# Attention and expert layer on one core: batch 0's value block sums by 128 queries, and a new listed order

## The chip, the cores and the metric

The kernel runs on one core of a Trainium2 chip. Its time is the device time in microseconds (us) of one execution. The core has five engines that each work through a list of their own, in order: PE (matrix products, with weight loads of its own, PEld), DVE and ACT (elementwise work and copies), POOL (here it issues loads) and SP (here it issues stores and moves). They wait for one another through semaphores.

## The reference, cut to what matters

Four batches of eight heads, 768 positions, head dimension 64. Each query sees its neighbours closer than 16 positions, and besides them 24 blocks of 32 keys, each by the maximum of its keys and the mean of its values. An expert layer follows on the 3072 x 512 result.

```python
def _attn_ref(q, k, v):
    k_sum = k.reshape(B, H, nb, block, D).max(axis=3)
    v_sum = v.reshape(B, H, nb, block, D).mean(axis=3)
    scores_l = scale * np.matmul(q, k.transpose(0, 1, 3, 2))
    mask_l = np.abs(pos[:, None] - pos[None, :]) < window
    scores_s = scale * np.einsum('bhsd,bhnd->bhsn', q, k_sum) + np.log(block)
    scores_all = np.concatenate([np.where(mask_l, scores_l, -1e9), scores_s], axis=-1)
    a = softmax(scores_all)
    return np.matmul(a, np.concatenate([v, v_sum], axis=2))

def _moe_ref(x, w_in, w_out):
    h = x @ w_in
    g = h * np.clip(h + 3.0, 0.0, 6.0) / 6.0
    return g @ w_out
```

## The kernel before

**Attention.** Queries go in blocks of 64 (12 of them, `NQ`). The keys of a block are its window of 96 positions (`WIN`) and, below them on partitions 96 to 119, the 24 block maxima: 120 rows in all (`KEYS`). `kaug` holds these keys, `vaug` the values in the same form, `qT` the queries, turned. Scores are products into a pair of PSUM banks `S`, `exp` on ACT makes `at` of them, and a product with `vaug`, which has a column of ones beside the 64 values, gives sums and divisor at once. `normal` (line 596) divides on DVE: a reciprocal `rc`, then `xn`. Transposes on PE and a copy give `x`, the expert layer's input, one tile for each half batch.

**Batch 0** starts the kernel and differs. Its heads go in four pairs `p`. Its late queries (the half called 0, `low` maps it) are scored first. `values_first` (line 567) makes the value products of that half in two steps, so that the first needn't wait for the block sums: `values1a` with the window's values, `values1b` with the block sums, which `vsum_first` (line 527) makes on PE and copies to `vf`. Both steps take 64 queries at a time, 12 products for a pair, in the two halves of the array's columns (`c`). The other half's queries come by wider loads, `qwide` (line 326), which PE transposes at line 442 (`q2`, `q3`) and DVE or ACT copy into `qT`.

**Expert layer.** A tile of 384 rows goes through 16 columns (`f1`): four products with `win` into a bank `h`, of which there are three, a relu on ACT into `r` (line 671), and a gate on DVE (line 672) into `g`. Then `f2` multiplies `g` with `wout` in three row blocks of four parts each into a bank `o` or `h`; a copy to `ot` and a store from SP end a block. The last row block of the last tile is cut into columns of 256, 128 and 128; one of the 128 is copied by ACT (line 698) and stored from ACT's own queue (line 699).

**Order.** Nothing is scheduled by the program itself: `ORDER` is a text of 977 tokens written out in the file, and `issue` (line 134) issues one operation for each. `v02.1` is the second operation of `values_first(2)`, `F0x3.0` the first of column 3 of tile 0, `G71x256.4` an operation of row block 1 of tile 7, `s`, `k`, `q`, `u`, `h`, `w` stand for scores, keys, queries, block sums, the values ahead of a block, and the turning of batches 1 to 3. `:A` or `:D` chooses ACT or DVE. So a token's place sets the order on its engine, and the PSUM banks and buffers are dealt out in that order too. `~`, `-`, `_` and `=` are products on a tile of ones (line 778) that keep PE at work.

Of the kernel before, what the change touches and what calls it, by code (L numbers as in the profile page):

```python
# [15 lines left out]
D = 64  # L16
BLK = 32
QB = 64
PAD = 16
WIN = QB + 2 * PAD  # L20
KEYS = 120
# [10 lines left out]
q0.1:A s000.1 q0.2:A =1 s010.0 s010.1 k2.2:A k3.2:D k3.3:D k3.1 V00.0 h000.0:D h001.0:D k2.1 k2.4 s000.2 ~2 =5 v00.0 V01.0 u0.0  # L32
h010.0:D s020.0 c.16 s010.2 q1.2:A u0.3:D u0.1:D u0.4:D v01.0 v01.1 v01.2 v00.1 q1.1:A V02.0 h020.0:A h021.0:A h011.0:A v00.2
s020.1 v01.3 v00.3 V03.0 u1.0 u1.3:A h030.0:D s030.0 k3.4 ~2 s030.1 u1.4:D v01.4 h031.0:D Q0w0.0 Q0w1.0 v01.5:D Q0w2.0 =1 q3.0
q3.1:D q2.0 u1.1:A u1.2:D s020.2 v02.0 v02.1 v02.2 s021.0 v02.3 s030.2 v03.0 v03.1 q2.1:A v03.2 s011.0 v03.3 v00.4 v00.5:D
v02.4 s021.1 s011.1 s021.2 v03.4 v03.5:D s011.2 v02.5:A s031.0 s031.1 s001.0 s031.2 I2.0 F0x3.0 F0x3.1 F0x3.2 F0x3.3 F0x3.4
F0x3.5 I4.0 F0x6.0 F0x6.1 F0x6.2 F0x4.0 F0x4.1 F0x4.2 F0x4.3 v411.0 v411.1 F0x5.0 F0x4.4 F0x4.5 v411.2 s001.1 I8.0 u0.2:A
s001.2 F0x8.0 F0x8.1 F0x8.2 F0x5.1 I0.0 F0x5.2 F0x11.0 F0x1.0 F0x11.1 F0x11.2 F0x1.1 F0x1.2 F0x1.3 F0x1.4 F0x1.5 v410.0 v410.1
F0x7.0 F0x7.1 F0x7.2 v410.2 F0x10.0 F0x10.1 I12.0 F0x13.0 F0x13.1 F0x15.0 F0x15.1 F0x13.2 F0x10.2 v411.3 v411.4:D v410.3
v410.4:A F0x15.2 F0x14.0 F0x14.1 F0x14.2 F0x9.0 F0x9.1 F0x9.2 F0x0.0 F0x0.1 F0x2.0 F0x2.1 K13.0 K10.0 c.12:A F0x0.2 K12.0 K11.0  # L40
w10.0 Q1w1.0 F1x14.0 F1x14.1 F1x14.2 F1x4.0 F1x4.1 F1x4.2 F1x2.0 F1x2.1 F1x2.2 w10.1:D F0x2.2 F0x2.3 F0x2.4 F0x12.0 F0x12.1
F0x12.2 F1x8.0 F1x8.1 F1x8.2 F1x1.0 F1x1.1 F1x1.2 F0x0.3 F0x0.4 F0x0.5 F0x2.5 F1x9.0 F1x9.1 F1x9.2 F1x5.0 F1x5.1 F1x5.2 F1x15.0
F1x15.1 w11.0 w11.2 F1x15.2 w11.3:D Q1w4.0 Q1w2.0 Q1w0.0 w10.2 w10.3:D q6.0 q6.1:A q7.0 q7.1:A F1x7.0 F1x7.1 w11.1:A F1x7.2
# [12 lines left out]
w22.1 v110.3 v110.4:A F2x7.0 F2x7.1 G11x0.2 F3x14.0 F3x14.1 F2x14.2 F2x7.2 F3x14.2 s200.0 s200.1 w23.1 w21.5:A s200.3 G11x0.3
F3x9.0 F3x9.1 F3x9.2 F3x8.0 F3x8.1 F3x8.2 F3x13.0 Q31.0 K31.0 s200.4 s200.2 G11x0.4:A G11x0.5 G12x0.5 s210.0 s210.3 s210.4
s210.1 s210.2 F3x4.0 F3x12.0 G22x0.0 F3x13.1 F3x13.2 H3.0 v201.0 K32.0 V32.0 w20.5:D F3x4.1 F3x4.2 V30.0 G00x0.5 F3x12.1 v200.0
v200.1 F3x2.0 v201.1 v201.2 v201.3 G22x0.1 F3x0.0 F3x0.1 G22x0.2 G22x0.3 w23.5:A G22x0.4:A F3x12.2 v200.2 v200.3 v201.5 F3x1.0
F3x1.1 F3x1.2 s201.0 w31.0 G20x0.0 v201.4 F3x0.2 F3x2.1 s201.3 F3x2.2 F3x11.0 s201.1 G20x0.1 F3x5.0 F3x11.1 F3x3.0 F3x5.1  # L60
F3x11.2 w30.0 F3x5.2 v201.7 F3x15.0 G20x0.2 F3x15.1 F3x15.2 w30.3 F3x3.1 F3x3.2 w22.5:A w30.4:D s201.4 F3x6.0 F3x6.1 H3.1:A
G20x0.3 G20x0.4:A F3x7.0 F3x10.0 G21x0.0 s211.0 F3x7.1 F3x10.1 s201.2 F3x7.2 s211.3 s211.1 F3x10.2 w32.0 F3x6.2 w32.3 s211.4
s211.2 w30.2:A G21x0.1 G21x0.2 G21x0.3 G21x0.4:A u6.0 u6.1:D u6.5:A u6.4:A u6.2:A w31.3 v211.0 v201.6 v210.0 v210.1 v210.2
w31.2:D v211.1 v210.3 v211.2 v211.3 G10x0.5 w31.4:D w33.0 G32x0.0 G32x0.1 G32x0.2 G32x0.3 G32x0.4:A F4x14.0 F4x14.1 F4x14.2
F4x4.0 F4x4.1 w32.2:A F4x4.2 F4x15.0 F4x15.1 F4x15.2 w31.1 G30x0.0 G30x0.1 F4x8.0 F4x8.1 F4x8.2 F4x2.0 F4x2.1 F4x2.2 F4x13.0
G30x0.2 F4x13.1 u6.3:A F4x13.2 w33.3 F4x7.0 F4x7.1 F4x7.2 G21x0.5 G20x0.5 v211.4 F4x6.0 F4x6.1 F4x6.2 v211.7 v211.6 v211.5
w30.1 F4x11.0 F4x11.1 F4x11.2 G30x0.3 G30x0.4:A G30x0.5 F4x1.0 F4x1.1 w33.2:A F4x1.2 w32.4:D F4x5.0 F4x5.1 F4x5.2 G22x0.5
# [95 lines left out]
def kernel(  # L163
# [74 lines left out]
    def bank(b, i=0):  # L238
        return b.slot[:, i] if any(b.slot is x for x in pairs) else b.slot[:]
# [570 lines left out]
```

## Time and profile before

| what | us |
|---|---|
| median of 3 runs | 216.8 |
| lowest and highest run | 216.46, 218.23 |
| span of the profiled execution, first to last instruction | 214.9 |
| PE busy in it | 208.8 |
| DVE busy | 162.7 |
| ACT busy | 135.9 |

The span is 1.9 us below the median of the runs, which also hold what lies around the first and last instruction; the profiled execution has no time of its own beside its span. Busy time of PE counts from the start of a product to its modelled end, and products overlap, so the spacing of their starts tells more than a mean length. A stretch's row gives its length, then busy time and count for PE, PEld, DVE, ACT and POOL, then the granted clock of PE, the load on the DMA engines and GB/s. A row of the timeline gives start, length, engine, line, what is written from what, and in brackets how long the engine stood idle before it and for whom.

### The profile page before, as it was taken

How to read it: one execution, taken by the hardware profiler on the slowest of the kernel's cores; microseconds unless marked ns; L12 is line 12 of the kernel's file. 1: busy time of each engine (PE TensorE's matmuls, PEld its weight loads, DVE VectorE, ACT ScalarE, POOL GpSimd, SP SyncE). 2: the span in 40 equal slices, each digit the busy share in tenths (PEclk: the TensorE clock that was granted, in tenths of full speed). 3: DMA queues.
4: the chain of work that ended last, by engine and by line, in shares of the span. 5: the costliest groups of instructions: out<-in, count | busy, mean ns of one | idle time of the engine just before them, and what ended most of it. 6: DMA issues, size and time to landing. Idle time of an engine off the chain costs nothing.

```text
span 214.9 us, 6125 instructions
## 1 busy us (share of the span) xinstructions
PE 208.8 (97%) x2564; PEld 119.7 (56%) x2564; DVE 162.7 (76%) x318; ACT 135.9 (63%) x264; POOL 49.5 (23%) x66
## 2 busy tenths in 40 slices
PE   7998999999999999999999999999999999999994
PEld 7566656555555565565555555555555555564443
DVE  6987999999899999898899889887865555550021
ACT  3987878887898988756578696566346355520110
POOL 7977358906643244000000000000000000000000
PEclk9999999999999999999999999999999999999999
DMA  5999999999999999930334234113314400113123
GB/s 75 159 155 189 203 188 170 190 203 162 206 160 187 181 135 151 108 146 11 38 37 143 28 37 110 49 21 39 70 19 81 78 0 3 49 49 122 52 80 139
DMA packets 91724, 22.68 MB, mean 106 GB/s; under 512 B 82224, under 2 KB 88752, under 8 KB 91696
## 3 DMA queue, kind: packets, MB, share of 16 engines
q0 software_dynamic: 62288, 14.41, 72.7%
q1 hardware_dynamic: 29264, 7.80, 15.4%
q8 instruction: 20, 0.33, 0.6%
q10 hardware_dynamic: 144, 0.07, 0.1%
q14 instruction: 8, 0.07, 0.1%
HBM read 28.82 MB, written 6.29 MB: 163 GB/s over the span
## 4 chain that ended last, share of the span: by engine, by line
PE 86%; POOL 5%; DMA 4%; DVE 1%; ACT 1%; issue 1%; POOLq 0%
PE h L667 38%; PE o L684 33%; PE h L684 5%; DMA qwide<-in_q_dram 4%; PE S L624 3%; PE S L513 3%; POOL vaug L344 2%; PE S L554 1%; ACT vaug L242 1%; POOL first L306 1%; PE S L637 1%; POOL qwide L326 1%; PE S L440 1%; PE S L667 1%; POOL first L313 1%; PE h L582 1%
## 5 line engine op out<-in xcount | busy, mean ns | idle before, releaser
L667 PE MATMUL h<-x,win 128*128 128x384 bf16 x500 | 91.1, 326 | 0.3 <-DVE g L672 0.3
L671 ACT ACTIVATE r<-h 128x384 f32<-128x384 f32 x125 | 58.7, 492 | 38.8 <-PE h L667 36.8
L672 DVE SCALAR_TENSOR_TENSOR g<-r,h 128x384 bf16<-128x384 f32 x125 | 65.7, 546 | 22.7 <-ACT r L671 20.1
L684 PE MATMUL o<-wout,g 128*128 128x512 bf16 x336 | 81.7, 379 | 0.0
L667 PEld LDWEIGHTS <-win 128*128 128x128 bf16 x512 | 48.7, 98 | 35.9 <-issue 0.5
L684 PEld LDWEIGHTS <-g 128*128 128x128 bf16 x416 | 38.7, 98 | 37.4 <-issue 0.3
L521 ACT ACTIVATE at<-S 120x768 bf16<-120x768 f32 x24 | 18.6, 811 | 5.5 <-PE S L513 5.4
L242 ACT COPY ot<-o 128x512 f32<-128x512 f32 x17 | 10.0, 586 | 15.4 <-PE o L684 14.2
L522 DVE TENSOR_TENSOR at<-at,mask 96x768 bf16<-96x768 bf16 x24 | 12.6, 549 | 2.0 <-ACT at L521 1.6
L606 DVE TENSOR_TENSOR xn<-S,rc 128x768 bf16<-128x768 f32 x14 | 13.3, 950 | 0.3
L242 DVE COPY ot<-h 128x512 f32<-128x512 f32 (+1 forms) x3 | 1.6, 555 | 14.3 <-PE h L684 14.3
L344 POOL DMA_DIRECT2D vaug<-in_v_dram x10 | 11.8, 1191 | 0.4 <-DMA first<-in_k_dram 0.2
L684 PE MATMUL h<-wout,g 128*128 128x128 bf16 (+2 forms) x80 | 11.4, 294 | 0.0
L468 DVE TENSOR_REDUCE red<-kaug 128x24 bf16<-128x768 bf16 x12 | 11.2, 942 | 0.1
L242 ACT COPY vaug<-vaug 32x640 bf16<-32x640 bf16 (+3 forms) x17 | 8.9, 574 | 0.8 <-DMA vaug<-in_v_dram 0.5
L242 ACT COPY vaug<-vs 24x1536 bf16<-24x1536 bf16 x6 | 8.8, 1468 | 0.6 <-DVE vs L242 0.5
L456 DVE STREAM_TRANSPOSE kaug<-kraw 128x768 bf16<-128x768 bf16 x8 | 8.1, 1020 | 0.3 <-PE S L513 0.3
L778 PE MATMUL o<-idle 128*128 128x64 bf16 (+2 forms) x70 | 7.0, 278 | 1.1 <-DVE idle L288 1.1
L334 POOL DMA_DIRECT2D kraw<-in_k_dram x8 | 5.9, 737 | 8.9 <-DVE kaug L456 7.3
L513 PEld LDWEIGHTS <-kaug 32*128 32x128 bf16 x576 | 5.3, 92 | 4.4 <-issue 3.6
L643 DVE STREAM_TRANSPOSE y<-xn 128x768 bf16<-128x768 bf16 x8 | 7.6, 964 | 0.2
L624 PEld LDWEIGHTS <-at 120*64 120x64 bf16 x336 | 6.2, 111 | 2.6 <-issue 1.5
(107 smaller groups left out, 183.6 us busy)
## 6 DMA issues: line engine op xcount, KB each, us to landing
out_dram<-ot SPq DMA_DIRECT2D x19, 256.0 KB, 2.3
vaug<-in_v_dram POOLq DMA_DIRECT2D x6, 384.0 KB, 13.1
wout<-in_moe_w_out_dram POOLq DMA_DIRECT2D x4, 512.0 KB, 9.9
win<-in_moe_w_in_dram POOLq DMA_DIRECT2D x3, 512.0 KB, 10.8
kraw<-in_k_dram POOLq DMA_DIRECT2D x8, 192.0 KB, 12.9
x<-y SPq DMA_DIRECT2D x64, 24.0 KB, 2.0
first<-in_k_dram POOLq DMA_DIRECT2D x6, 192.0 KB, 12.3
first<-in_q_dram POOLq DMA_DIRECT2D x6, 192.0 KB, 12.3
```

What stands on the lines that cost most here:

```text
L242: {"ACT": nc.scalar.copy, "DVE": nc.vector.tensor_copy, "POOL": nc.gpsimd.tensor_copy}[eng](o, i)
L344: op("POOL", "dma128", lambda: nc.gpsimd.dma_start(out=o[BLK:WIN, a:z, 0:D], in_=rows[:, a:z]), w=[("v", b % 2, c) for c in range(lo, hi)] ...
L468: op("DVE", "max", lambda: nc.vector.tensor_reduce(red.slot[:], w[:, :, BLK:WIN].rearrange("p t (n c) -> p t n c", n=2), axis=AX.X, op=ALU ...
L513: nc.tensor.matmul(X[g // 2].slot[:, g % 2, i * QB:(i + 1) * QB], kaug[2 * u + m][rows, t], qT[rows, 2 * u + m, t * QB:(t + 1) * QB], star ...
L521: op("ACT", "exp", lambda a=a, e=e: nc.scalar.activation(a, X[e].slot[0:KEYS, :, 0:HALF], AF.Exp, scale=scl), r=[X[e]], w=[("at", p, half)])
L522: op("DVE", "masking", lambda m=m: nc.vector.tensor_tensor(m, m, mask[:, low(half):low(half) + HQ].unsqueeze(1).to_broadcast([WIN, 2, HQ, ...
L606: nc.vector.tensor_tensor(o, src[..., 0:D], r.unsqueeze(len(r.shape)).to_broadcast(list(o.shape)), op=ALU.mult)
L624: nc.tensor.matmul(X.slot[64 * c:64 * c + 64, i, m:m + D + 1], a[:, t * QB:(t + 1) * QB], vaug[b % 2][0:KEYS, h, t, 0:D + 1], start=True, ...
L667: nc.tensor.matmul(bank(h)[:, 0:HALF], w_in_sb[:, kt, cols], xt[s].slot[:, kt], start=(kt == 0), stop=(kt == NP - 1))
L671: op("ACT", "relu", lambda: nc.scalar.activation(r.slot[:], bank(h)[:, 0:HALF], AF.Relu, bias=0.5, scale=1.0 / 6.0), r=[h], w=[r])
L672: op("DVE", "gate", lambda: nc.vector.scalar_tensor_tensor(gt[s].slot[:, ft], r.slot[:], 1.0, bank(h)[:, 0:HALF], op0=ALU.min, op1=ALU.mul ...
L684: nc.tensor.matmul(o.slot[:, a:z], gt[s].slot[:, ft, ts * 128:(ts + 1) * 128], w_out_sb[:, ft, a:z], start=(ft == 0), stop=(ft == NFT - 1))
```

## The change

`values1b` takes 128 queries at once: six products for a pair in place of twelve, each with weights 128 columns wide. This needs the two blocks of 64 queries to lie side by side, which they do, since a block's number is `(2 * T + c + HQ) % NQ`. The window's products stay as they were.

```diff
-        def mms(rows, sums):
+        def own():
             for T in range(3):
                 for h in range(2):
                     for c in range(2):
-                        y, t, cols = each(T, h, c)
-                        w = vf[p][rows, h, 0:D + 1] if sums else vaug[0][rows, 2 * p + h, t, 0:D + 1]
-                        nc.tensor.matmul(y, at[p][rows, h, cols], w, start=not sums and T == h == 0, stop=sums and T == 2 and h == 1)
-        op("PE", "values1a", lambda: mms(slice(0, WIN), False), r=[("at", p, 0), ("v", 0, p), ("vh", 0, p, 0)], w=[X])
-        op("PE", "values1b", lambda: mms(slice(WIN, KEYS), True), r=[("vf", p)], w=[X])
+                        t = (2 * T + c + HQ) % NQ
+                        nc.tensor.matmul(bank(X)[64 * c:64 * c + 64, part(T, h)], at[p][0:WIN, h, t * QB:(t + 1) * QB],
+                                         vaug[0][0:WIN, 2 * p + h, t, 0:D + 1], start=T == h == 0, stop=False)
+
+        def summed():
+            for T in range(3):
+                for h in range(2):
+                    lo = (2 * T + HQ) % NQ * QB
+                    nc.tensor.matmul(bank(X)[:, part(T, h)], at[p][WIN:KEYS, h, lo:lo + 2 * QB], vf[p][WIN:KEYS, h, 0:D + 1],
+                                     start=False, stop=T == 2 and h == 1)
+        op("PE", "values1a", own, r=[("at", p, 0), ("v", 0, p), ("vh", 0, p, 0)], w=[X])
+        op("PE", "values1b", summed, r=[("vf", p)], w=[X])
```

`part(T, h)` is the slice of 65 columns that `each` named before. Besides, the table of tokens is another from its sixth line to its end; of it:

```diff
-s020.1 v01.3 v00.3 V03.0 u1.0 u1.3:A h030.0:D s030.0 k3.4 ~2 s030.1 u1.4:D v01.4 h031.0:D Q0w0.0 Q0w1.0 v01.5:D Q0w2.0 =1 q3.0
+s030.2 v02.1 u1.3:A v01.4 q3.0 v02.2 q2.0 v02.3 q3.1:D q2.1:D u0.2:D v01.5:A v00.5:A v03.0 s021.0 h031.0:A v03.1 s011.0 I12.0
```

The loads of batch 0 and of the weights stand in the same order on POOL, as do the products on ones in number; the loads of batches 1 to 3 and the stores come in another order.

On PE, around the transposes of `qwide` in batch 0. One row of each group of products is shown: `at` by its pair's number, `vf` the block sums, `xn` what is transposed into `x`. Before:

```order
L490 MATMUL S1_89<-qT_68,kaug3_67 128x64
...
L590 MATMUL h0_90<-ident_82,xn0_103 128x128
...
L442 MATMUL h2_92<-ident_82,qwide_78 128x128
...
L582 MATMUL h0_90<-vaug0_76,at2_74 64x65
...
L582 MATMUL h0_90<-vf_79,at2_74 64x65
...
L582 MATMUL h2_92<-vaug0_76,at3_75 64x65
```

With the change:

```order
L490 MATMUL S0_88<-qT_68,kaug3_67 128x64
...
L580 MATMUL h0_90<-vaug0_76,at2_74 64x65
...
L596 MATMUL h1_91<-ident_82,xn0_103 128x128
...
L587 MATMUL h0_90<-vf_79,at2_74 128x65
...
L596 MATMUL h2_92<-ident_82,xn1_104 128x128
...
L442 MATMUL S1_89<-ident_82,qwide_78 128x128
...
L580 MATMUL o0_93<-vaug0_76,at3_75 64x65
```

Pair 2's two value steps and one more set of transposes moved ahead of the late queries.

On DVE, from the scaling ahead of those queries' copies to the first masking. Here `qT` is the copy of the late queries, `rc` and `xn` the division, `x` the expert layer's input. Before:

```order
L242 COPY x0_97<-h0_90 128x384
L242 COPY qT_68<-h2_92 128x2x384
L242 COPY vaug0_76<-vf_79 24x2x6x64
L599 RECIPROCAL rc2_112<-h0_90 128x6
L606 TENSOR_TENSOR xn2_105<-h0_90,rc2_112 128x384
L599 RECIPROCAL rc0_110<-h2_92 128x6
L606 TENSOR_TENSOR xn0_103<-h2_92,rc0_110 128x384
L242 COPY x0_97<-o0_93 128x384
L498 TENSOR_TENSOR at2_74<-at2_74,mask_83 96x2x384
```

With the change:

```order
L605 RECIPROCAL rc2_112<-h0_90 128x6
L612 TENSOR_TENSOR xn2_105<-h0_90,rc2_112 128x384
L242 COPY qT_68<-S1_89 128x2x384
L242 COPY qT_68<-S0_88 128x2x384
L242 COPY vaug0_76<-vf_79 24x2x6x64
L605 RECIPROCAL rc0_110<-o0_93 128x6
L612 TENSOR_TENSOR xn0_103<-o0_93,rc0_110 128x384
L242 COPY x0_97<-h0_90 128x384
L242 COPY vaug0_76<-vf_79 24x2x6x64
L242 COPY x0_97<-h1_91 128x384
L498 TENSOR_TENSOR at2_74<-at2_74,mask_83 96x2x384
```

Both copies into `qT` are DVE's now, and pair 2's division moved ahead of them.

At the program's end, on SP, the stores of the last row blocks. Before:

```order
L694 DMA out_dram<-ot_122 16x512
L695 DMA out_dram<-ot_122 112x512
L695 DMA out_dram<-ot_120 128x512
L695 DMA out_dram<-ot_121 128x512
L695 DMA out_dram<-ot_122 128x128
```

With the change:

```order
L701 DMA out_dram<-ot_121 128x128
L700 DMA out_dram<-ot_122 16x512
L701 DMA out_dram<-ot_122 112x512
L700 DMA out_dram<-ot_119 16x512
L701 DMA out_dram<-ot_119 112x512
L701 DMA out_dram<-ot_121 128x256
L701 DMA out_dram<-ot_120 128x512
```

SP's last store is a whole row block of 256 KB now. The one of 128 columns on ACT's queue, which stood ahead of SP's last store, is now the last store of the program.

113 lines of the change are left out of this document (56 added, 57 removed).

## Prediction

> **What bounds the kernel now.** I read the page first, then the groups by line with shapes kept apart, the stretches of 10 us, the chain of waits, and last the timelines of PE and DVE at the places where the change moves work. From the page:
>
> ```profile
> span 214.9 us, 6125 instructions
> PE 208.8 (97%) x2564; PEld 119.7 (56%) x2564; DVE 162.7 (76%) x318; ACT 135.9 (63%) x264; POOL 49.5 (23%) x66
> PEclk9999999999999999999999999999999999999999
> PE 86%; POOL 5%; DMA 4%; DVE 1%; ACT 1%; issue 1%; POOLq 0%
> ```
>
> PE is busy for 97% of the span, at the full granted clock, and carries 86% of the chain that ended last. So what there is to win is PE's idle time, 214.9 - 208.8 = 6.1 us, and PE work that is dropped. The stretches say where the idle time is:
>
> ```profile
> 0.00:10.00 10.00, 8.62 (x134) 6.37 (x134) 7.75 (x27) 6.43 (x11) 8.64 (x19) 1.00 0.83 113
> 10.00:20.00 10.00, 9.21 (x205) 5.85 (x199) 8.72 (x25) 8.78 (x19) 8.26 (x11) 1.00 2.19 166
> 20.00:30.00 10.00, 9.52 (x192) 6.56 (x193) 8.59 (x20) 8.20 (x14) 4.06 (x5) 1.00 1.36 201
> 40.00:50.00 10.00, 9.79 (x187) 5.73 (x187) 9.68 (x18) 8.53 (x17) 3.02 (x4) 1.00 1.52 195
> 60.00:70.00 10.00, 9.89 (x150) 5.81 (x149) 9.69 (x16) 8.97 (x17) 3.95 (x6) 1.00 2.28 175
> 80.00:90.00 10.00, 10.00 (x108) 5.62 (x107) 9.86 (x16) 8.15 (x20) 2.94 (x3) 1.00 2.07 139
> 210.00:214.90 4.90, 1.92 (x30) 1.63 (x28) 0.98 (x2) 0.27 (x1) 0.00 (x0) 1.00 0.33 118
> ```
>
> The first number behind a stretch's length is PE's busy time, the third DVE's. Of the 6.1 us idle, 1.38 lie in the first 10 us, which the change leaves as they are, and 2.98 behind PE's last product, which no order of PE's work fills. What the new order can reach is 0.79 + 0.48 in 10 to 30 us, and 0.21 + 0.11 and little more later. DVE stands at 9.69 to 9.86 of 10 us between 40 and 90 us, beside a PE that hardly waits: DVE has little room there.
>
> The one wait that stands out is at the late queries of batch 0, `qwide`. The timeline of PE, and the chain of waits:
>
> ```profile
> 19.02 0.34 PE L590 MATMUL h<-ident,xn 128*128 128x128 bf16 x3
> 19.23 0.28 PE L442 MATMUL h<-ident,qwide 128*128 128x128 bf16 x2
> 20.31 0.73 PE L442 MATMUL h<-ident,qwide 128*128 128x128 bf16 x10 [0.81 <-DMA qwide<-in_q_dram]
> 20.97 0.38 PE L582 MATMUL h<-vaug,at 96*64 96x65 bf16 x12
> 21.28 0.38 PE L582 MATMUL h<-vf,at 24*64 24x65 bf16 x12
> 21.59 0.35 PE L490 MATMUL S<-qT,kaug 64*128 64x64 bf16 x12
> 24.17 0.34 PE L667 MATMUL h<-x,win 128*128 128x384 bf16 x1
> ```
>
> ```profile
> 12.02 8.25 DMA qwide<-in_q_dram
> ```
>
> The last piece of `qwide` lands at 12.02 + 8.25 = 20.27 us; PE takes it at 20.31. The twelve transposes are through at 20.97, and the first product of the expert layer starts at 24.17. POOL's queue is the same in both kernels up to the loads of `win` and of batch 1's keys, so 20.27 stays.
>
> **The change part by part.**
>
> *The value block sums.* 48 products of 64 queries become 24 of 128. The rows:
>
> ```profile
> L582 PE MATMUL h<-vf,at 24*64 24x65 bf16 x48 | 1.5, 193 | 0.1
> L778 PE MATMUL o<-idle 128*128 128x64 bf16 x40 | 2.3, 242 | 1.1 <-DVE idle L288 1.1
> L684 PEld LDWEIGHTS <-g 128*128 128x128 bf16 x416 | 38.7, 98 | 37.4 <-issue 0.3
> ```
>
> Half the products is not half the time. A group of twelve takes 21.59 - 21.28 = 0.31 us from its start to that of the next work, 26 ns for each, since two of them (one for each half of the array's columns) run at once. The nearest row for the new form, weights 128 wide with 64 columns streamed, is the idle product at 2.3 / 40 = 57 ns: six of these are 0.34 us. So a group goes from 0.31 to about 0.34, and at best, if a wide product costs what a narrow one does, to 6 x 0.026 = 0.16. Four groups: between -0.6 and, if the change of shape (it lies within the 0.31) comes on top of the 0.34, some +0.5 us. I take 0: the idle row is the nearest, and three of the four groups stand ahead of the landing at 20.27, which PE waits for anyway, the fourth beside the DVE chain below. If that cover is gone, 4 x 0.03 = 0.1 us is the price.
>
> A rule of the Trainium skill speaks against the wide form. The page "TensorE: Matmul & The Clock Gate", Part 3, "The mechanism", says that a weight load overlaps running products only when its row group differs, and here all 24 lie on the same rows; its section on LDWEIGHTS gives columns / 1.2 ns, which is 107 ns for 128. By the page, as an estimate, 24 x (107 + 27) = 3.2 us would replace 1.2. The idle row shows otherwise: its loads are 128 wide on the same rows each time, and it comes to 57 ns in all.
>
> *The wait for `qwide`.* The new order puts more ahead of it: of pair 2 both value products, 0.31 + 0.31, and one more set of three transposes, about 0.2 (19.02 to 19.23 in the rows, with one idle product in it). That is 0.8 us into a hole that lasts from about 19.3 to 20.3. PE is then 0.8 us less behind at 20.97, but this is not all won: DVE is late next. The prices on DVE and ACT:
>
> ```profile
> L242 DVE COPY qT<-h 128x768 bf16<-128x768 bf16 x1 | 0.6, 558 | 0.9 <-PE h L442 0.9
> L242 ACT COPY qT<-h 128x768 bf16<-128x768 bf16 x1 | 0.8, 798 | 1.1 <-PE h L442 1.1
> L242 DVE COPY vaug<-vf 24x768 bf16<-24x768 bf16 x3 | 1.2, 394 | 0.1
> L599 DVE RECIPROCAL rc<-h 128x6 f32<-128x6 f32 x4 | 0.7, 186 | 0.1
> L606 DVE TENSOR_TENSOR xn<-h,rc 128x384 bf16<-128x384 f32 x4 | 2.1, 555 | 0.1
> L242 DVE COPY x<-h 128x384 bf16<-128x384 bf16 x2 | 0.7, 342 | 0.0
> ```
>
> ```profile
> 20.75 0.56 DVE L242 COPY qT<-h 128x768 bf16<-128x768 bf16 x1 [0.87 <-PE h L442]
> ```
>
> Before, DVE starts its copy of the late queries at 20.75 and ACT makes the second copy, 0.80 us, at the same time. Now both are DVE's. From 20.75 on its list is, up to the last copy into `x` that the first expert product needs: two copies into `qT` (1.12), a spread of `vf` (0.39), reciprocal (0.19), scaling (0.56), a copy into `x` (0.34), a spread (0.39), a copy into `x` (0.34): 3.33 us, so 24.08. The fourth product of the first expert column, the one that reads it, then starts at about 24.1 to 24.4. Before it started at 24.17 + 3 x 0.16 = 24.66. PE's own list is through a little after 24.1 as well, since its last scores wait for the bank that an exp on ACT frees. I take a gain of 0.3 us; the ends are 0 (DVE slips by another copy) and 0.8 (all that was moved).
>
> *The first expert columns, 24 to 42 us.* Here three banks `h` go round between product, ACT's relu and DVE's gate. One wait of note is in the trace, of 40.21 - 39.59 - 0.16 = 0.46 us:
>
> ```profile
> 39.59 0.33 PE L667 MATMUL S<-x,win 128*128 128x384 bf16 x1
> 40.21 2.11 PE L667 MATMUL h<-x,win 128*128 128x384 bf16 x12 [0.30 <-DVE g L672]
> ```
>
> ```profile
> L672 DVE SCALAR_TENSOR_TENSOR g<-r,h 128x384 bf16<-128x384 f32 x125 | 65.7, 546 | 22.7 <-ACT r L671 20.1
> L456 DVE STREAM_TRANSPOSE kaug<-kraw 128x768 bf16<-128x768 bf16 x8 | 8.1, 1020 | 0.3 <-PE S L513 0.3
> ```
>
> It is DVE's: a block transpose of batch 1's keys, 1.02 us, stands between two gates, each 65.7 / 125 = 0.53 us, while one expert column is 4 x 0.16 = 0.65 us of PE. The new list has the same pattern, with the second such transpose ahead of the gate that frees the bank of the second last column before the late queries' transposes. I expect the same wait in another place: 0, between -0.46 (gone) and +0.5 (one more).
>
> *Batches 1 to 3, 42 to 205 us.* PE hardly idles, so moving work wins at most 0.3 us here. It can lose: DVE at 9.7 to 9.9 of 10 has room for 0.1 to 0.3 us of lateness. The new list spreads gates and second-layer products more evenly and lets DVE's turns come later, which speaks against new waits; the list is new all the way, which speaks for a few. I take +0.2, between -0.3 and +1.4 (three waits like that of 0.46).
>
> *The end.* Before, the last product's quarter of a row block is copied by DVE and stored from SP; now by ACT and stored from ACT's queue, and a 256 KB store goes out from SP just before.
>
> ```profile
> 211.11 0.27 ACT L698 COPY ot<-h 128x128 f32<-128x128 f32 x1 [5.26 <-PE h L684]
> 211.96 0.29 DVE L242 COPY ot<-h 128x128 f32<-128x128 f32 x1 [0.82 <-PE h L684]
> ```
>
> ```profile
> out_dram<-ot SPq DMA_DIRECT2D x19, 256.0 KB, 2.3
> out_dram<-ot ACTq DMA_DIRECT2D x1, 64.0 KB, 2.1
> out_dram<-ot SPq DMA_DIRECT2D x1, 64.0 KB, 1.6
> ```
>
> Copies of 0.27 to 0.29 us are alike; the store is 2.1 us in place of 1.6. The 256 KB block now ends only three groups of four short products (0.7 us) ahead of PE's end, so its copy (0.6) and store (2.3) end 2.2 us behind PE, just under 0.3 + 2.1. That is +0.5 us, between 0 (ACT's store lands as SP's did) and +0.7. The Trainium skill, "DMA: Bandwidth & Descriptors", section "Issuing engines are not separate DMA queues", says that stores from either engine run on the same 16 DMA engines, so by it this term would be 0 and the sum 216.7. The rows say 2.1 and 1.6, each with other transfers beside it, and I go by them.
>
> **Sum:** 0 - 0.3 + 0 + 0.2 + 0.5 = +0.4, a span of 215.3 us. The profiled span is 1.9 us under the median of the runs (216.8), which I keep: 217.2 us.
>
> **The rivals.**
> - *The holes close* (faster). PE's reachable idle time is 0.79 + 0.48 + 0.21 + 0.11 = 1.6 us, and with 0.6 from the block sums 2.2: 214.6 us, if the end costs nothing. Against it: 20.27 stays and DVE's chain of 3.33 us behind it.
> - *DVE falls behind in batch 1* (slower). Between 40 and 90 us a gate that comes late holds a bank `h`, and PE's next expert column with it. Each such wait costs about 0.46 us. Without the 0.2 of the sum the forecast is 217.0; it decides from five waits on, 217.0 + 5 x 0.46 = 219.3 us. For it: DVE's 9.86 of 10 us. Against it: the more even spread.
> - *The weight loads are not hidden* (slower). Were each of the 24 wide loads, 98 ns in the row above, to stand uncovered ahead of its product of 57 ns, they would take 24 x 0.155 = 3.7 us in place of 1.2, all between 16 and 24 us: 217.2 + 2.5 = 219.7 us. Against it: the idle row, whose loads are hidden. It is the page on TensorE of the Trainium skill that speaks for it.
> - *Nothing comes of it*: the moved work only trades one wait for another and the end is as before, 216.8 us.
>
> **How the numbers follow.** A measurement of this kernel tells about 1% from no change, that is 214.6 and 219.0. My forecast together with "nothing comes of it" has 0.74, the closing of the holes 0.09, DVE's lateness 0.13, the serial loads 0.04. The likeliest case is 217.2, its own range 215.8 to 218.8 by the ends of the terms (gains rarely all come together). The range for 8 in 10 reaches towards both other cases, 215.2 to 219.3. So faster 0.09, same 0.74, slower 0.17.
>
> **What would show it.** Right: L442's wait for `qwide` under 0.2 us; the fourth product of the first expert column at about 24.3; the 24 wide products at 50 to 60 ns; PE's idle time in 30 to 200 us still under 1 us; the last store landing about 0.5 us later behind PE's end. Wrong: PE waiting for `g` or `xn` at several places between 40 and 90 us, a wide product at over 100 ns, or PE's first expert product well before 24 us.

## The result, and the profile after

The changed kernel takes 219.49 us (median of four runs, 218.93 to 220.16), the kernel before beside it 216.81 us (216.46 to 218.23): the ratio is 1.0111, with a 95% interval of 1.0077 to 1.0146. It is slower by 1.1%. The forecast was 217.2 us, in a range from 215.2 to 219.3. The median lies 0.2 us above that range; the ratio, taken on 216.81 us, gives 219.2 us, just inside its upper end. A second measurement on another chip (the first experiment below) gave 1.0098 (1.0065 to 1.0131), 219.03 us. The ratios compare whole sets of runs, so they differ a little from the quotient of two medians.

The page of the changed kernel, with the lines that answer to those shown of the kernel before:

```profile
span 218.2 us, 6050 instructions
PE 207.4 (95%) x2512; PEld 119.5 (55%) x2540; DVE 163.5 (75%) x322; ACT 128.2 (59%) x260; POOL 49.1 (23%) x66
```

PE has 24 products less to do and DVE as much as before (163.5 against 162.7 us), and yet the span is 3.3 us longer. 28 of the 2540 products are missing in this trace (x2512 beside x2540 loads of weights), so its stretches look idler than they were. The profile of the second measurement (span 217.1 us) has them all, and its stretches of 10 us are the ones to compare:

```profile
10.00:20.00 10.00, 9.75 (x225) 6.39 (x219) 9.25 (x26) 7.52 (x16) 8.14 (x11) 1.00 2.19 166
20.00:30.00 10.00, 9.66 (x163) 6.25 (x164) 9.55 (x24) 8.16 (x17) 3.80 (x5) 1.00 1.36 200
60.00:70.00 10.00, 8.81 (x129) 5.00 (x129) 9.63 (x18) 3.36 (x8) 3.18 (x4) 1.00 2.09 189
80.00:90.00 10.00, 9.42 (x139) 5.58 (x133) 9.13 (x18) 7.58 (x18) 6.80 (x7) 1.00 1.18 95
210.00:217.10 7.10, 3.74 (x34) 2.44 (x31) 0.42 (x1) 0.86 (x3) 0.00 (x0) 1.00 0.31 102
```

The first 30 us went as hoped: PE is busy for 9.75 and 9.66 us where it was 9.21 and 9.52. What was won there is lost between 60 and 70 us (8.81 in place of 9.89) and between 80 and 90 us (9.42 in place of 10.00). Behind PE's last product the program now takes 7.10 - 3.74 = 3.36 us in place of 2.98. The view of waits names what PE waited for between 40 and 120 us in the second profile (us in total, times, the longest); the first has the same five at 0.3 to 0.8 us:

```profile
PE S L630 <- DVE vaug L242: 1.2, 2, 0.8
PE S L513 <- DVE x L242: 0.6, 1, 0.6
PE S L643 <- DVE xn L612: 0.3, 1, 0.3
PE h L673 <- DVE vaug L242: 0.3, 1, 0.3
```

Five waits, 2.4 us. Measured from one product's start to the next, and with the usual distance taken off, they come to 0.54 + 0.98 + 0.44 + 0.77 + 0.44 = 3.2 us. The view puts all five down to DVE, and for the first four that is right. The last one is at 116.65 us, where PE begins to use a new tile of `x`. That tile is filled by SP's moves `x<-y`, and the last of them landed at 116.19, 0.46 us before PE went on. In all seven profiles of the new order PE goes on 0.46 us behind that landing, while the end of DVE's copy shifts against it. So this wait of 0.44 us is for the moves, and 2.7 us are left for DVE.

Two of the four stand inside the value products of batch 1 (L630), which need DVE's spreads of the block sums (`vaug<-vs`). PE there, in the second profile:

```profile
60.10 0.57 PE L630 MATMUL S<-vaug,at 120*64 120x65 bf16 x24 [0.38 <-DVE vaug L242]
61.48 0.38 PE L630 MATMUL S<-vaug,at 120*64 120x65 bf16 x12 [0.81 <-DVE vaug L242]
```

DVE and POOL at that place, in the first profile of the changed kernel (its times run about 0.7 us later):

```profile
58.66 3.46 DVE L242 COPY vaug<-vs 24x1536 bf16<-24x1536 bf16 x3 [0.32 <-ACT vs L242]
```

```profile
53.15 0.71 POOL L334 DMA_DIRECT2D first<-in_q_dram  x1 [2.08 <-DMA vaug<-in_v_dram]
55.49 0.71 POOL L334 DMA_DIRECT2D first<-in_q_dram  x1 [1.64 <-DMA vaug<-in_v_dram]
56.91 1.34 POOL L344 DMA_DIRECT2D vaug<-in_v_dram  x1 [0.71 <-ACT at L521]
58.24 0.71 POOL L334 DMA_DIRECT2D first<-in_q_dram  x1
59.03 1.34 POOL L353 DMA_DIRECT2D vaug<-in_v_dram  x1
60.37 1.36 POOL L344 DMA_DIRECT2D vaug<-in_v_dram  x1
```

And in the kernel before:

```profile
58.94 1.82 DVE L242 COPY vaug<-vs 24x1536 bf16<-24x1536 bf16 x3
```

```profile
51.88 1.34 POOL L344 DMA_DIRECT2D vaug<-in_v_dram  x1
53.21 1.40 POOL L353 DMA_DIRECT2D vaug<-in_v_dram  x1
55.24 0.73 POOL L334 DMA_DIRECT2D first<-in_q_dram  x1 [0.63 <-DMA vaug<-in_v_dram]
56.22 1.34 POOL L344 DMA_DIRECT2D vaug<-in_v_dram  x1 [0.24 <-DMA first<-in_k_dram]
```

Here H2 (L353) and V20 (the last L344 of each view) are loads of batch 2's values; the first figure of such a token is the batch. The same three copies take 3.46 us in place of 1.82. One by one they are 0.68, 1.36 and 1.35 us. The second starts at 59.37, while POOL issues the load H2 (59.03 to 60.37), the third at 60.77, while it issues V20 (60.37 to 61.73), and each ends 0.4 us behind that issue. In the kernel before, H2 (53.21) and V20 (56.22) were issued by 57.56, ahead of the spreads. In the new listed order two loads of queries stand ahead of batch 2's first load of values in POOL's queue, and each waits 1.6 to 2.1 us for an earlier load, so all that follows comes later. At 88 us the same thing is seen once more, with the load V32:

```profile
88.00 1.11 DVE L242 COPY kaug<-red 128x288 bf16<-128x288 bf16 x1
...
89.72 0.56 DVE L242 COPY x<-S 128x768 bf16<-128x768 bf16 x1
```

```profile
87.72 1.34 POOL L344 DMA_DIRECT2D vaug<-in_v_dram  x1
```

This copy takes 0.19 to 0.24 us where no issue is in its way. The copy into `x` behind it is what PE's scores of batch 2 wait for.

One more thing stands out in the first profile: a pause in which PE waits for nothing that the trace shows, ahead of the last of the twelve transposes of the late queries, whose data had landed.

```profile
20.06 0.78 PE L442 MATMUL S<-ident,qwide 128*128 128x128 bf16 x11
21.43 0.22 PE L442 MATMUL S<-ident,qwide 128*128 128x128 bf16 x1 [0.59 <-issue]
```

So the theory is: **a DVE copy from SBUF to SBUF doesn't go on while POOL issues a load, the new order puts POOL's issues beside such copies, and these copies are on PE's path.** The rivals: DVE's list is simply too full there; the wide products cost more than they save; the time of a single profile is an accident; the transfers themselves, and not their issue, slow the copies.

### The profile page after: what moved, and what is told of

It reads as the page before. It is cut to its first block, busy times and chain, and to the rows that moved or that the text cites. A ratio compares the mean times of both kernels' runs of the same rounds, so it can differ in the third digit from the quotient of the medians.

```text
span 218.2 us, 6050 instructions
## 1 busy us (share of the span) xinstructions
PE 207.4 (95%) x2512; PEld 119.5 (55%) x2540; DVE 163.5 (75%) x322; ACT 128.2 (59%) x260; POOL 49.1 (23%) x66
## 4 chain that ended last, share of the span: by engine, by line
PE 80%; DVE 11%; DMA 3%; issue 2%; POOL 2%; ACT 1%; DVEq 0%; POOLq 0%
PE h L673 35%; PE o L690 28%; PE h L690 5%; DMA first<-in_q_dram 3%; DVE vaug L242 2%; PE S L513 2%; PE S L630 2%; DVE g L678 2%; DVE kaug L456 1%; DVE xn L612 1%; POOL first L306 1%; PE S L673 1%; DVE qT L460 1%; DVE at L522 1%; DVE red L468 1%
## 5 line engine op out<-in xcount | busy, mean ns | idle before, releaser
L673 PE MATMUL h<-x,win 128*128 128x384 bf16 x500 | 92.3, 326 | 0.5 <-DVE vaug L242 0.5
L677 ACT ACTIVATE r<-h 128x384 f32<-128x384 f32 x125 | 59.5, 491 | 48.1 <-PE h L673 46.0
L690 PE MATMUL o<-wout,g 128*128 128x512 bf16 x309 | 79.2, 379 | 2.2 <-issue 1.1
L242 ACT COPY ot<-o 128x512 f32<-128x512 f32 x18 | 10.5, 586 | 14.7 <-PE o L690 13.8
L344 POOL DMA_DIRECT2D vaug<-in_v_dram x10 | 11.9, 1190 | 19.5 <-PE S L630 18.1
L690 PE MATMUL h<-wout,g 128*128 128x512 bf16 (+2 forms) x79 | 11.2, 293 | 0.1
L630 PE MATMUL S<-vaug,at 120*64 120x65 bf16 x336 | 7.4, 196 | 1.2 <-DVE vaug L242 1.2
L630 PEld LDWEIGHTS <-at 120*64 120x64 bf16 x336 | 6.3, 111 | 3.7 <-issue 2.7
L784 PEld LDWEIGHTS <-idle 128*128 128x128 bf16 x80 | 5.7, 124 | 3.1 <-DVE idle L288 1.1
L513 PE MATMUL S<-qT,kaug 32*128 32x64 bf16 x576 | 6.8, 190 | 0.6 <-DVE x L242 0.6
```

The source lines that it names most:

```text
L242: {"ACT": nc.scalar.copy, "DVE": nc.vector.tensor_copy, "POOL": nc.gpsimd.tensor_copy}[eng](o, i)
L513: nc.tensor.matmul(X[g // 2].slot[:, g % 2, i * QB:(i + 1) * QB], kaug[2 * u + m][rows, t], qT[rows, 2 * u + m, t * QB:(t + 1) * QB], star ...
L630: nc.tensor.matmul(X.slot[64 * c:64 * c + 64, i, m:m + D + 1], a[:, t * QB:(t + 1) * QB], vaug[b % 2][0:KEYS, h, t, 0:D + 1], start=True, ...
L673: nc.tensor.matmul(bank(h)[:, 0:HALF], w_in_sb[:, kt, cols], xt[s].slot[:, kt], start=(kt == 0), stop=(kt == NP - 1))
L677: op("ACT", "relu", lambda: nc.scalar.activation(r.slot[:], bank(h)[:, 0:HALF], AF.Relu, bias=0.5, scale=1.0 / 6.0), r=[h], w=[r])
L690: nc.tensor.matmul(o.slot[:, a:z], gt[s].slot[:, ft, ts * 128:(ts + 1) * 128], w_out_sb[:, ft, a:z], start=(ft == 0), stop=(ft == NFT - 1))
```

## The experiments

**The changed kernel once more**, unedited. Expected:

> The changed kernel once more, with nothing edited, so that its waits can be told from those of a single execution. If the lateness at 60 us belongs to the program (the copies vaug<-vs of batch 1 at 0.68, 1.36 and 1.35 us in its first profile, beside POOL's issue of two loads), they are long again and the ratio is 1.011 +- 0.004, about 219.5 us. If it was an accident of that one profile, the copies take about 0.55 us and PE waits less than 0.5 us between 58 and 64 us. The gap of 0.76 us ahead of the last transpose of the late queries at 20.67 us shall show in the same way whether it comes again.

Measured: 219.03 us, ratio 1.0098 (1.0065 to 1.0131). The three spreads take 0.72, 1.37 and 1.35 us, the waits are those shown above, and PE's wait for the last transposes of the late queries is now for the data (0.42 us), with no pause behind it. The lateness at 60 and 88 us belongs to the program. The pause at 20.6 us does not come each time.

**The new order with the narrow products.** The body of `values_first` is that of the kernel before; the listed order is the new one.

> The new listed order, but the products with value block sums by 64 queries as before (48 products in place of 24). If the order is the cause: as the changed kernel, 219.5 +- 0.4 us, since the four groups of products cost the same in either form to within 0.1 us each. If the wide products are the cause (weight loads that are not hidden): back to 217.0 +- 0.5 us.

Measured: 221.26 us, ratio 1.0199 (1.0149 to 1.025). Neither: the narrow products make the new order slower by another 2.2 us. The timeline of PE shows a pause in the middle of a group of twelve products, and the stretches of 2 us show what it did to the clock (third number from the right):

```profile
19.07 0.34 PE L582 MATMUL h<-vf,at 24*64 24x65 bf16 x9
20.83 0.24 PE L582 MATMUL h<-vf,at 24*64 24x65 bf16 x3 [1.42 <-issue]
```

```profile
22.00:24.00 2.00, 1.95 (x52) 1.66 (x52) 1.65 (x5) 1.90 (x5) 0.66 (x2) 0.54 1.24 206
24.00:26.00 2.00, 2.00 (x33) 1.37 (x31) 1.65 (x5) 0.98 (x2) 0.17 (x1) 0.50 1.35 199
26.00:28.00 2.00, 2.00 (x7) 0.94 (x8) 1.75 (x4) 0.99 (x2) 1.13 (x2) 0.50 1.28 210
28.00:30.00 2.00, 2.00 (x32) 1.01 (x30) 0.82 (x3) 1.26 (x3) 0.58 (x1) 0.76 1.62 183
```

PE stands for 1.42 us, and 1.3 us later its clock is granted at half for 2 x (0.46 + 0.50 + 0.50 + 0.24) / 0.5 = 6.8 us, which costs 3.4 us of PE's work. The value products that stand between the first expert columns start at 29.1 us, in the repeat of the changed kernel at 25.5. Of these 3.6 us the kernel gets back 1.4 in batch 1, where DVE is no longer late for PE (0.14 and 0.45 us lost between 63 and 67 us in place of 0.54 + 0.98 + 0.44). The narrow form alone isn't dear: two groups of twelve in a row take 0.50 us at 16.9 us, where two wide groups of six take 0.47 in the repeat of the changed kernel. What the pause is, a later experiment asks.

**The old order with the wide products.** The listed order of the kernel before, with the new `values_first`.

> The old listed order with the products by 128 queries (24 in place of 48). If the order is the cause: as the kernel before, 216.8 +- 0.5 us, and the four groups at 0.25 to 0.35 us each. If the wide products are the cause: 218.5 us or more, with PE behind by 20 to 24 us into the program.

Measured: 216.14 us beside 216.62 us, ratio 0.9972 (0.9951 to 0.9993). That is 0.2 us under the range expected for "the order is the cause". The wide products don't cost, the order does. They even win a little, 0.6 us with an interval of 0.15 to 1.1. The rows explain 0.1 of it: a group of six takes 0.28 to 0.29 us in place of 0.31. Where the rest is from was not found.

**POOL held back at 60 us.** In the changed kernel POOL makes a copy of a few elements ahead of the load H2, from what DVE's spreads write, so that it waits for them:

```diff
 def load_ahead(b):
 ...
+    def go():
+        if b == 2:
+            nc.gpsimd.tensor_copy(seen[WIN:KEYS], vaug[1][WIN:KEYS, :, 0, 0])
+        nc.gpsimd.dma_start(out=o[0:BLK, 1:n, 0:D], in_=rows[QB - BLK:QB, 0:n - 1])
```

> The changed kernel, with one small copy on POOL ahead of the loads H2 and V20 of batch 2 that reads what DVE writes in batch 1's last spread: POOL then issues the two loads behind DVE's spreads and not beside them. If DVE's copies are stretched because POOL issues loads at the same time, and if that is on the path: the three copies back to about 0.55 us, the waits of the value products of batch 1 (0.50 and 0.98 us in the changed kernel) mostly gone, about 218.0 us (1.3 to 1.7 us less). If DVE's list is late there for another reason: the copies as long as before or the waits as long, 219.5 +- 0.4 us; if the later loads are then missed by batch 2, more than 219.5.

Measured: 217.54 us, ratio 1.0041 (1.0014 to 1.0069), 1.5 us less than the changed kernel beside it, within the 1.3 to 1.7 us expected. The timelines of DVE, POOL and PE:

```profile
58.28 1.81 DVE L243 COPY vaug<-vs 24x1536 bf16<-24x1536 bf16 x3 [0.32 <-ACT vs L243]
```

```profile
60.25 0.25 POOL L356 COPY seen<-vaug 24x8 bf16<-24x8 bf16 x1 [1.71 <-DVE vaug L243]
60.73 1.35 POOL L357 DMA_DIRECT2D vaug<-in_v_dram  x1 [0.23 <-issue]
```

```profile
59.70 0.95 PE L635 MATMUL S<-vaug,at 120*64 120x65 bf16 x48
```

The three spreads are back at 1.81 us with nothing else on DVE's list changed, and PE does its 48 value products in one go. "DVE's list is too full" falls for this place.

**POOL held back at 86 us as well**, in the same way, ahead of V32 (`if b == 3 and lo == 2`, reading what batch 2's spreads write):

> The kernel with POOL held back at 60 us (217.54 us), and POOL held back in the same way ahead of V32, the last load of batch 3's values, until DVE has spread batch 2's block sums. Theory (DVE's copies between SBUF tiles don't go on while POOL issues a load): the copy kaug<-red at 86 us takes about 0.2 us in place of 1.14, PE's wait of 0.61 us ahead of batch 2's scores goes, 216.9 +- 0.4 us. Rival (DVE's list is simply full there): the copy or the wait stays, 217.5.

Measured: ratio 1.0009 (0.998 to 1.0038), 217.01 us beside 217.14 us on this chip. The copy and the scores that waited:

```profile
88.02 0.23 DVE L243 COPY kaug<-red 128x288 bf16<-128x288 bf16 x1
```

```profile
89.55 0.55 PE L522 MATMUL S<-qT,kaug 32*128 32x64 bf16 x48
```

The copy takes 0.23 us and the 48 scores run without a stop. The ratio falls by 0.0032, 0.7 us, as expected; the two ratios come from different chips and their intervals overlap, so that the size rests on the profiles (a wait of 0.8 us at this place, gone) more than on the measurement.

**The end.** The last quarter of a row block goes back to DVE and SP, the quarter with ACT's store is moved ahead, and the 256 KB block ends two groups earlier. The end of the list (further up, `G71x256` takes the places of `G71x384`):

```diff
-... G60x0.1 G71x0.2 G70x0.4:A G60x0.2 G71x0.3 G71x256.0 G70x0.5 G60x0.3 G71x256.1 G60x0.4:A G71x0.4:D
-G71x0.5 G60x0.5 G71x256.2 G71x256.3 G71x256.4
+... G60x0.1 G70x0.4:A G60x0.2 G70x0.5 G60x0.3 G60x0.4:A G60x0.5 G71x0.2 G71x0.3 G71x0.4:D G71x0.5
+G71x384.0 G71x384.1 G71x384.2 G71x384.3 G71x384.4:D G71x384.5
```

> The kernel with POOL held back at both places, and the end of the listed order changed: the quarter that ACT copies and stores is moved ahead, the last quarter is copied by DVE and stored from SP as in the kernel before, and the 256 KB block ends two groups earlier. If the store from ACT's queue and the late 256 KB block are what the end costs: from PE's last product to the end of the span 2.96 us or a little less in place of 3.37, 0.4 us less than the same kernel without it. If the end is set by the transfers whatever queue issues them: 3.3 us or more, no change. In all about 216.5 us, which would be the kernel before.

Measured: ratio 0.9967 (0.9942 to 0.9993), 216.34 us beside 217.14 us. The last stretch, first without the edit, then with it:

```profile
210.00:216.90 6.90, 3.53 (x33) 2.33 (x30) 0.42 (x1) 0.85 (x2) 0.00 (x0) 1.00 0.32 105
```

```profile
210.00:214.90 4.90, 1.90 (x25) 1.64 (x23) 0.72 (x2) 0.58 (x1) 0.00 (x0) 1.00 0.32 112
```

Behind PE's last product stand 6.90 - 3.53 = 3.37 and 4.90 - 1.90 = 3.00 us: 0.37 us, as expected. Which of the three changes wins it is not shown: ACT's last store took 2.0 us to land (213.86 to 215.86) beside a 256 KB store issued 0.3 us before it, SP's takes 1.5 us (212.31 to 213.86) beside one of half that size, issued 0.8 us before it. The ratio falls by 0.0042, 0.9 us, with intervals that again overlap. With the three edits the new order beats the kernel before by 0.3%, as the old order with the wide products does (0.9972).

**The wait at 40 us in the kernel before.** The old order with the wide products, and POOL held ahead of V10 until DVE's copy `kaug<-kaug` is written (`if b == 1 and lo == 0: nc.gpsimd.tensor_copy(seen, kaug[0][:, 1:9, 0])`):

> The old listed order with the products by 128 queries (216.14 us), and POOL held back ahead of the load V10 until DVE's copy kaug<-kaug at 39 us is written. In the kernel before that copy took 1.12 us beside POOL's issue of V10, against 0.25 elsewhere, and PE waited 0.46 us for the gate behind it at 40.2 us. Theory: the copy at 0.25 us, the wait at 40.2 us gone, 215.7 +- 0.4 us. Rival: the wait is due to the block transpose of 1.02 us, as the prediction had it, and stays: 216.1; or V10 lands too late for the halo copies at 54 us: more than 216.1.

Measured: ratio 0.9965 (0.9942 to 0.9987). DVE in the kernel before, where POOL issues V10 from 38.21 to 39.57, then DVE and PE in this one:

```profile
38.51 1.19 DVE L242 COPY kaug<-kaug 128x352 bf16<-128x352 bf16 x2
```

```profile
38.17 0.50 DVE L243 COPY kaug<-kaug 128x352 bf16<-128x352 bf16 x2
```

```profile
39.25 0.33 PE L678 MATMUL S<-x,win 128*128 128x384 bf16 x1
39.41 2.11 PE L678 MATMUL h<-x,win 128*128 128x384 bf16 x12
```

The two copies take 0.50 us in place of 1.19, and the wait of 0.46 us behind the product at 39.25 is gone. So the block transpose of 1.02 us, to which the prediction put that wait down, was not what made it. In the old order with wide products and V10 not held, the two copies took 1.03 us and PE lost 0.30 us there. In the time the cure doesn't show: 0.9965 and 0.9972 can't be told apart. Nor does every execution of the old order have the wait. In the profiles of the next two runs, which leave V10 alone, DVE's first copy began when V10's issue was 1.2 us old, took 0.25 us, and PE lost nothing. The overlap depends on a few tenths of a us.

**The cost put into the kernel before.** V20's issue is held back until the first of the three spreads is written (`if b == 2 and lo == 0`, reading the first spread's rows):

> The kernel before, with the suspected cost put in: POOL's issue of V20 (56.2 us in the kernel before) is held until DVE has written the first of batch 1's three spreads, so that it falls beside the other two. Theory: one of the other two spreads takes 1.2 to 1.4 us in place of 0.55 to 0.67, PE waits 0.3 to 0.8 us more at the value products of batch 1, 217.0 to 217.5 us. Rival (POOL's issue costs DVE nothing, and what was long in the changed kernel had another cause): spreads at 0.55 to 0.7 us, 216.6.

Measured: ratio 0.9983 (0.9955 to 1.0011), and the spreads stay as they were. But the test missed its aim. The timelines of DVE and POOL:

```profile
59.51 1.72 DVE L243 COPY vaug<-vs 24x1536 bf16<-24x1536 bf16 x3
```

```profile
60.13 0.57 POOL L347 COPY seen<-vaug 24x2 bf16<-24x2 bf16 x1 [3.77 <-DVE vaug L243]
60.64 1.57 POOL L348 DMA_DIRECT2D vaug<-in_v_dram  x1
```

POOL's copy of two elements a row took 0.57 us, and its issue 1.57 us in place of 1.34. Here DVE was there first, and POOL was the one to wait. So the next run lets POOL begin earlier.

**The same with POOL first**: V20 is held only until the halo copy ahead of the spreads is written.

> The kernel before again with POOL's issue of V20 held, now only until DVE's halo copy ahead of the spreads (58.9 to 59.3 us) is written, so that POOL's issue begins beside the first spread and not behind the second, as in the changed kernel. In the run before this one POOL came last: its own small copy took 0.57 us and its issue 1.57 in place of 1.34, and the spreads stayed at 0.55. Theory (DVE's copies and POOL's issues exclude each other, and who comes first goes first): the second spread waits until POOL's issue of 1.34 us has ended and takes 1.2 to 1.4 us, the spreads end 0.6 to 0.8 us later, PE waits for them at the value products of batch 1, and the ratio to the kernel before is 1.001 to 1.004. Rival (in the changed kernel the spreads were long for another reason): all three spreads at 0.55 to 0.68 us, ratio 0.998 to 1.001.

Measured: ratio 1.0019 (1.0002 to 1.0037). DVE, POOL and PE:

```profile
58.98 2.61 DVE L243 COPY vaug<-vs 24x1536 bf16<-24x1536 bf16 x3
```

```profile
59.06 1.45 POOL L348 DMA_DIRECT2D vaug<-in_v_dram  x1
```

```profile
61.12 0.60 PE L629 MATMUL S<-vaug,at 120*64 120x65 bf16 x26
62.24 0.54 PE L629 MATMUL S<-vaug,at 120*64 120x65 bf16 x22 [0.51 <-DVE at L527]
```

The second spread, started at 59.55, took 1.32 us and ended 0.36 us behind POOL's issue; the three take 2.61 us in place of 1.82, and PE stops in its value products as it does in the changed kernel. The kernel before gets the illness of the changed one from the time at which POOL issues one load, and the loads behind it in its queue. In time that is about 0.4 us, with an interval that barely clears zero, so the profile carries this more than the ratio.

The twelve profiles together also decide the last rival. They hold 212 DVE copies between SBUF tiles that begin while POOL issues a load. The 81 that begin in the first 0.24 us of the issue all kept their usual duration. The other 131 all ended with the issue (0.03 us ahead of its end at the earliest) or behind it, though 70 of them would have been through inside it at their usual duration. Where such a copy is held, its end stands behind the issue's end by a distance of its own: 0.36 to 0.39 us for a spread, 0.03 to 0.07 for `kaug<-red`. The transfers of these loads land 7 us and more after their issue at the median (changed kernel, second profile), so a copy slowed by the transfer would not end there.

**What the pause at 20 us is.** The new order with the narrow products again, with nine more idle products early on, of the same length in all (`~12` becomes `~9 -12`):

> The new order with products by 64 queries (221.26 us), and nine more idle products early on (nine long ones and twelve short ones where twelve long ones stood, of the same length in all). In the three profiles that show it, PE stops between its 350th or 351st product and the next, whatever work that is. If it waits there for the next piece of its own program: the pause of 1.4 us comes nine products earlier in the listed work, between the transposes of pair 1 and the value block sums of pair 2, still behind about 350 products, the clock falls to half behind it again, 221.3 +- 0.7 us. If the pause belongs to that work (the value block sums, their bank or their data): it stays behind the ninth of the twelve products.

Measured: ratio 1.0179 (1.0101 to 1.0256), 221.38 us. The timeline of PE, and the clock behind it:

```profile
19.05 0.34 PE L590 MATMUL h<-ident,xn 128*128 128x128 bf16 x3
20.68 0.54 PE L582 MATMUL h<-vf,at 24*64 24x65 bf16 x12 [1.29 <-ACT vf L242]
```

```profile
22.00:24.00 2.00, 2.00 (x41) 1.64 (x41) 1.52 (x4) 1.47 (x5) 0.58 (x2) 0.50 1.25 206
```

The pause stands nine products earlier in the listed work, exactly. (The profile puts it down to ACT's copy into `vf`, but that ended at 19.94, 0.74 us before PE went on.) What stays the same is the number of products ahead of it:

| kernel | products ahead | PE stops, goes on | behind which work | 16 KB of program landed |
|---|---|---|---|---|
| changed | 350 | 20.61, 21.43 | 11th of 12 transposes of the late queries | 19.82 |
| changed, POOL held at 60 us | 350 | 19.98, 20.93 | the same | 19.51 |
| new order, narrow | 351 | 19.22, 20.83 | 9th of 12 block sums of pair 2 | 19.37 |
| the same, nine idle products more | 351 | 19.17, 20.68 | transposes of pair 1 | 19.05 |
| before, V20 held, first run | 350 | 20.95, 21.61 | a product in a group of twelve value products | 20.00 |
| before, V20 held, second run | 350 | 20.43, 21.09 | the same | 19.49 |

(Products are counted in each trace by their starts.) The last column is the end of the one packet of the queue that the page calls "instruction" and that moves 16 KB between 18 and 20 us; PE goes on 1.4 to 1.6 us behind it in each. (In the two kernels with POOL held twice the pause is shorter, 0.3 to 0.4 us, also behind 350 products, 1.2 and 1.5 us behind the packet.) In the repeat of the changed kernel the packet ended at 19.03 and PE came to its 350th product at 20.63, 1.60 us later, and did not stop; in the kernel before it came there at 21.09, 2.07 us behind. So PE waits for the next piece of its own program. Why that piece is fetched so late was not tried.

The three kernels with POOL held meet such a border once more, at their 989th product. The first of them:

```profile
61.16 1.67 PE L695 MATMUL o<-wout,g 128*128 128x512 bf16 x7 [0.19 <-issue]
```

From start to start PE loses 0.36 to 0.39 us there in the three, each time 1.5 us behind the end of another packet of 16 KB. That PE, rid of its waits for DVE, comes to this border sooner is likely but was not tested.

## Why the prediction was right or wrong

The sum said +0.4 us, and +2.1 to +2.4 was measured. That the time lies at the upper end of the range is owed to the range, which was stretched towards a rival, and not to the terms of the sum.

- **The failed step is "Batches 1 to 3, 42 to 205 us"**: +0.2 us, between -0.3 and +1.4. It measured 3.2 us of new waits, less 0.27 at 60 us that is gone: about +2.9. The step looked at DVE's list ("the new list spreads gates and second-layer products more evenly") and priced a wait at 0.46 us, a gate that comes late. It didn't ask what can lengthen DVE's copies, and compared POOL's queue only "up to the loads of `win` and of batch 1's keys". Behind that point the new order moves POOL's issues of H2, V20 and V32 by 4 to 7.5 us, onto DVE's copies. One such collision makes a copy of 0.19 to 0.55 us one of 1.1 to 1.4 us. The row was there in the kernel before: the copy `kaug<-kaug` of 0.25 us had taken 1.12 at 38.51, under an issue of POOL. Of the 3.2 us, 2.7 are waits for DVE behind such copies, and 0.44 is the wait for SP's moves.
- **The rival "DVE falls behind in batch 1"** (0.13) is the case that came nearest, with 219.3 us against 219.5 and 219.0, but the number is luck: it counted five gates at 0.46 us. Its reason was not the one that came: DVE was late because it was locked out, not because it was full. With POOL held at both places, the same list in the same order shows no wait for DVE between 40 and 115 us. The rival's row was also misread: DVE stands at 9.68 to 9.86 of 10 us in three of the five stretches between 40 and 90 us, and at 9.02 and 9.22 in those at 50 and 70 us.
- **The wait for `qwide`**, -0.3 us (0 to -0.8): under 0.2 us was forecast, and 0.42 for the data or a pause of 0.59 us were seen. The moved work did come ahead of it, but PE then meets the end of the loaded program at its 350th product, at about the same time as the data. The first two products of the first expert column now start at 22.2 to 23.1 us, well before 24, which was named as a sign of being wrong; the fourth starts at 24.66 in the first profile and at 23.93 in the second, against 24.67 before. The gain is 0 to 0.7 us: the term and its bounds hold, though its small wait did not come.
- **The value block sums**, 0 (-0.6 to +0.5): right. A wide product takes 0.28 / 6 = 47 ns, group of six, beside the 50 to 60 forecast, so the weight loads are hidden and the third rival falls. That the form matters for another reason was in no part of the prediction: with three wide groups ahead of PE's 350th product there are 18 products less in front of that border, and in the new order that is worth 2.2 us.
- **The first expert columns**, 0 (-0.46 to +0.5): the wait of 0.46 us is gone, the lower end. It was put down to a block transpose; the run with POOL held at V10 shows that it was POOL's issue beside DVE's copy.
- **The end**, +0.5: measured 3.36 - 2.98 = 0.38 us in the second profile and 0.37 us in the run that undoes it. Whether the queue or the 256 KB block beside it makes the last store slower stays open.

The sum by what was measured, second profile against the one before: start -0.7, the waits at 40 and 60 us that went -0.7, the new waits +3.2, the end +0.4, in all +2.2 us. The spans differ by 217.1 - 214.9 = 2.2 us. From span to time the prediction added 1.9 us; every run that lists both has 1.7 to 1.8 (219.9 and 218.2), so its span of 215.3 stands for 217.0 us.

The rows bear out a rule of the Trainium skill that the prediction left out. "SBUF — State Buffer", section "Who interferes with whom", says that DVE's second pair of SBUF ports is shared with GpSimd under an exclusive lock, held for a whole instruction. The trace agrees in both directions: a spread of 0.55 us took 1.32 to 1.37 us with POOL first, and a copy of two elements a row on POOL took 0.57 us with DVE first, in place of 0.17.

## What to carry to other kernels

When an order changes, follow the queue that issues the loads to its end, not only the engines that compute: a load that is issued a few us later can be hidden as a transfer and still cost, by what its issue does to the engine beside it. Look for copies of one shape with two durations, and lay the other engines' timelines beside the long ones; a small dependent instruction ahead of the issue tests it, and cures it, here for 0.2 to 0.5 us of an engine with time to spare. A stop in PE that stands behind the same number of instructions in different programs belongs to the program's loading and not to the work, so fewer instructions ahead of it can be worth more than their own time.

## What the hardware showed that was not expected

- A DVE copy between SBUF tiles that starts more than 0.24 us into POOL's issue of a load ends with that issue or up to 0.4 us behind it, in all 131 cases of the twelve profiles: 0.55 to 1.36 us (60 us), 0.19 to 1.11 (88 us), 0.25 to 1.12 (39 us, kernel before). One that starts earlier in the issue is not held (81 cases). DVE's other work kept its duration beside such issues: the gates, which read PSUM, at 0.55 us, but also the masking products at 0.55 and the block transposes at 1.03, which stay within SBUF.
- A pause of PE of 1.3 to 1.4 us came with a clock that was halved for 6.8 us, 3.4 us of work, in both kernels that show it: from 1.3 us behind the pause in one, from 0.3 us before its end in the other. Seven of their eight runs have a mean clock of 0.975 to 0.990. Pauses of 0.4 to 0.8 us left it at 1.00. The Trainium skill, "TensorE: Matmul & The Clock Gate", section "Why this matters for your kernels", asks for gaps of more than about 3 us for that; here less than half did it, and the measurement decides.
- PE can outrun the loading of its own program: where its products take 26 to 56 ns, it stood for 0.3 to 1.5 us behind the 350th, and went on 1.2 to 1.6 us behind the packet of 16 KB.
